# Attention and experts in one kernel: values stored block by block, shorter tables, and adding transfers placed after a gather

## Chip, cores and metric

The kernel runs on one core of a Trainium2 chip. The metric is device time in microseconds of one execution. The engines are TensorE (PE, with its weight loads as PEld), VectorE (DVE), ScalarE (ACT), GpSimd (POOL) and SyncE (SP), which here only issues transfers.

## What is computed

Windowed attention over 8 batches, 8 heads, 576 positions and 64 dims, and then a mixture of experts over the 4608 tokens, where each of 8 experts takes exactly 576 tokens by global greedy choice:

```python
mask_plain = (rel >= 0) & (rel < 32)                          # heads 0 to 3
mask_dil = (rel >= 0) & (rel < 128) & (rel % 4 == 0)          # heads 4 to 7
attn = softmax(where(mask, q @ k.T / 8, -1e9))
x = (attn @ v).transpose(0, 2, 1, 3).reshape(4608, 512)
logits = x @ w_gate                                           # 8 experts
# all (token, expert) pairs in order of falling logit: a pair is taken
# if the token is free and the expert has fewer than 576 tokens
for e in range(8):
    out[mask_e] = relu(x[mask_e] @ w1[e]) @ w2[e]             # 512 -> 1024 -> 512
```

## The kernel before

**Attention** works in 32 units: 8 batches times two kinds of heads (kind 0 plain, kind 1 dilated) times two halves. For a kind the positions are cut into query blocks (9 of 64 plain, 3 of 48 per residue dilated), each with its key block of 96 or 80 positions, 32 of which overlap the block before. A unit (class `Unit`, from L389) scans scores in bf16 for the row maxima (`scan`, L486, and `most`, L493), makes exact scores with the mask and maxima folded in by table matmuls (`scores`, L503 and L506), takes the exponential on ACT (L456), multiplies by the values (`values`, L514) and normalises on DVE (`weigh`). The result goes to the DRAM tensor `xd`; transposes (L564) and matmuls make the gate logits.

The values stand in SBUF with keys of a block on the partitions: 96 rows by 9 blocks by 4 heads by 65 numbers (plain) and 80 rows by 3 blocks by 4 residues by 4 heads by 65 (dilated). `load_v` (L280) loads them for one batch and kind with two transfers, the first block and then the others, from a DRAM layout by position: each row of a block is one contiguous run of 1040 B (plain) or 4160 B (dilated). `load` (L343) brings queries and keys, in 128 rows; for batch 0 in two halves each, and ACT, DVE or POOL copy the queries into a zero-padded tile.

Tables come by `load_const` (L1450): 0 is the identity and masks in bf16, 1 and 2 are the selection tables `lsel0` and `lsel1` for the two kinds (128 rows, of which `scores` reads 64 plus the number of blocks of the unit: 73 or 76), and call 3 loads three together: the fp32 identity, the bf16 tables of the choices (`tri` and on) and the fp32 tables of the choices (`pri` and on). The choices of a batch (`coarse`, L642) read them.

**Experts** (`moe`) run in 8 rounds. Round r finds the expert that fills next by a search on PE and DVE, lists its tokens, gathers their 512 numbers from `xd` by five indirect transfers on POOL (`gather`, L1250; L1258), transposes them on PE (L1272), and splits them into a high and a low part. GEMM 1 (L1309) and GEMM 2 (L1351) use three products of high and low parts. `weights` (L1144) loads a raw tile of 128 x 512 fp32 and splits it: ACT makes the high part, and DVE the low part by a subtraction. For the pairs in `ADDED`, round 0's w2 and round 1's w1 and w2, ACT writes the negated high part and a POOL-issued transfer adds the raw tile to it (L1169). Eight raw tiles of w1 serve in turn; a one-element memset on POOL (L1150), tied to a gather, holds back part of a round's raw loads.

**Order.** Each phase is written out by a list planner (`Schedule`). Every operation has an engine, a planned cost in ns, dependencies, and a boost that moves its due time; the planner takes the operation that is due first on the engine that is free first, and emits the instructions in that order. Each engine then executes in that order, waiting on semaphores for data. Loads on SP get boosts that fall by 1e6 from one call of `sp` (L303) to the next, so they keep the order in which the program names them; the planner takes a transfer to need its bytes divided by `D_R` = 262 B/ns.

Of the kernel before, what the change touches and what calls it, by code (L numbers as in the profile page):

```python
# [14 lines left out]
OP = mybir.AluOpType  # L15
# [4 lines left out]
B, H, S, D = 8, 8, 576, 64  # L20
# [4 lines left out]
WIN, DIL = 32, 4  # L25
NB = S // 64
SR = S // DIL
# [4 lines left out]
NM = 5  # L32
# [6 lines left out]
B_L, B_G, B_T, B_X, B_H, B_HL, B_Y, B_S, B_W = 23000, 27000, 15000, 0, 20000, 17000, 28000, -15000, 1500  # L39
RAW1, D_R, NQ, AHEAD_W = 8, 262, (2, 2), (3, 4)  # L40
ADDED, T_A, T_G = (("2", 0), ("1", 1), ("2", 1)), 4500, 4500
# [7 lines left out]
def blocks(kind):  # L49

    if kind == 0:
        return [(64 * c, max(0, 64 * c - 32)) for c in range(NB)]
    return [(48 * c, max(0, 48 * c - 32)) for c in range(3)]
# [3 lines left out]
KB = (96, 80)  # L57
# [98 lines left out]
class Schedule:  # L156
# [8 lines left out]
    def op(self, eng, cost, fn, deps=(), boost=0, lat=0, dma=0, buf=None):  # L165
        x = Op(len(self.ops), eng, cost, fn, deps, boost, lat, dma, buf)
        for d in x.deps:
            d.users.append(x)
        self.ops.append(x)
        return x  # L170
# [72 lines left out]
def attention(tc, ctx, C, load_const, T, xd, Lt, R):  # L243
    nc = tc.nc
# [5 lines left out]
    op = K.op  # L250
# [27 lines left out]
        return t.rearrange("p (h c a i) -> p h c a i", h=8, c=3, a=2)  # L278

    def load_v(b, kind):  # L280
        n, w, st, q, src = ((96, NB, S, 64, T["in_vp"]), (80, 3, SR, 48, T["in_vd"]))[kind]
        row = src.shape[2]
        t = VT[kind][:n, b % 2]
        t = t.rearrange("p c h d -> p c (h d)") if kind == 0 else t.rearrange("p c r h d -> p c (r h d)")
        o = src.offset + b * st * row
        nc.sync.dma_start(t[:, 0], bass.AP(tensor=src.tensor, offset=o, ap=[[row, n], [1, row]]))
        nc.sync.dma_start(t[:, 1:], bass.AP(tensor=src.tensor, offset=o + (q - 32) * row,
                                            ap=[[row, n], [q * row, w - 1], [1, row]]))


    users = {}
# [10 lines left out]
    first = [1e8]  # L302

    def sp(cost, fn, deps, bytes_, b):
        first[0] -= 1e6
        return op("SP", 475 * cost, fn, deps, first[0], dma=bytes_ / D_R)

    def const(i):
        ready["c", i] = sp(1 if i < 3 else 3, lambda: load_const(i), (), 128 * 1500, 0)

    ready = {}

# [68 lines left out]
    class Unit:  # L381
# [37 lines left out]
        def op(self, eng, cost, fn, deps, boost=0, buf=None):  # L419
            return op(eng, cost, fn, deps, boost - self.u * P_U, buf=buf)  # L420
# [222 lines left out]
    def coarse(c0, c1, x, late):  # L643
        for c in range(c0, c1):
            g, used, use_ = PRE.take()
            f = op("DVE", 290, lambda c=c, g=g: R.coarse(c, g), [x, *used], late)
            counted[0] = op("PE", 60, lambda c=c, g=g: R.coarse_counts(c, g), [f, ready["c", 3], counted[0]], late)
            use_.append(counted[0])

    def tokens(un):  # L650
# [39 lines left out]
    counted = [None]  # L690
# [28 lines left out]
    load(0, 1, 1)  # L719
    load_values(0, 1)  # L720
    const(3)

    def gate_weights():
        nc.gpsimd.memset(wgp, 0.0)
# [386 lines left out]
def moe(tc, ctx, C, R, xd, w1, w2, out):  # L1111
# [33 lines left out]
    def weights(n, r, f, deps):  # L1145

        raw, old, use = RAW[n].take()
        if n == "1" and r < len(AHEAD_W) and f == AHEAD_W[r]:

            gate[r] = op("POOL", 100, lambda: nc.gpsimd.memset(raw[:1, :1], 0.0), [got[r, 1], *old], B_G)  # L1150
        if r in gate:
            deps = [*deps, gate[r]]

        def load():
            if n == "1":
                src = w1[bass.ds(E[r], 1), f].rearrange("o p d f -> p (o d f)")
            else:
                src = w2[bass.ds(E[r], 1), f * 128:f * 128 + 128, :].rearrange("o p d -> p (o d)")
            nc.sync.dma_start(raw, src)

        ld = op("SP", 60, load, [*deps, *old], dma=T_W)
        h, oldh, useh = WH[n].take()
        l, oldl, usel = WL[n].take()
        hi = op("ACT", 525, lambda: act(h, raw), [ld, *oldh], B_W)
        if (n, r) in ADDED:
            use.append(hi)
            ne = op("ACT", 525, lambda: nc.scalar.activation(l, h.bitcast(F32), AF.Copy, scale=-1.0), [hi, *oldl], B_W)
            useh.append(ne)
            lo = op("POOL", 1040, lambda: nc.gpsimd.dma_start(l, raw, accum_op=OP.add), [ne], B_W, lat=T_A)  # L1169
            use.append(lo)  # L1170
        else:
            lo = op("DVE", 600, lambda: sub(nc.vector, l, raw, h), [ld, hi, *oldl], B_W)
            use += [hi, lo]
        useh.append(lo)
        return h, l, hi, lo, useh, usel
# [239 lines left out]
def layout(inputs):  # L1415

    q, k, v, w1, w2 = (np.asarray(inputs[n]) for n in ("q", "k", "v", "moe_w1", "moe_w2"))
    plain = lambda x: x[:, :4].reshape(B, 2, 2, S, D).transpose(0, 1, 4, 2, 3).reshape(B, 128, 2, S)
    dilated = lambda x: x[:, 4:].reshape(B, 4, SR, 2, 2, D).transpose(0, 4, 5, 1, 3, 2).reshape(B, 128, 4, 2, SR)
    ones = lambda x: np.concatenate([x, np.ones(x.shape[:-1] + (1,), x.dtype)], -1)  # L1420
    cb, _, cf, _ = consts()
    rows = np.where(np.arange(24 * 4 * (D + 1)) % (D + 1) == D, 1e-9, 0.0).astype(np.float32)
    d = {
        "in_qp": plain(q), "in_kp": plain(k),
        "in_qd": dilated(q).reshape(B, 128, 8, SR), "in_kd": dilated(k),
        "in_vp": ones(v[:, :4].transpose(0, 2, 1, 3)).reshape(B, S, 4 * (D + 1)),
        "in_vd": ones(v[:, 4:].transpose(0, 2, 1, 3)).reshape(B, SR, DIL * 4 * (D + 1)),
        "in_moe_w_gate": np.asarray(inputs["moe_w_gate"]),
        "in_moe_w1": w1.reshape(NE, DM // 128, 128, FF // 128, 128).transpose(0, 3, 2, 1, 4),
        "in_moe_w2": w2,  # L1430
        "in_cb": cb, "in_cf": cf, "in_rows": np.stack([rows, np.ones_like(rows)]),
    }
    return {n: np.ascontiguousarray(a) for n, a in d.items()}


def load_consts(tc, pool, T):

    nc = tc.nc
    _, ob, _, of = consts()
    cb, cf = T["in_cb"], T["in_cf"]  # L1440
    C, parts = {}, []
    cuts = [(cb, BF, ob, "ident", "lsel0"), (cb, BF, ob, "lsel0", "lsel1"), (cb, BF, ob, "lsel1", "rsel0"),
            (cf, F32, of, "identf", "pri"), (cb, BF, ob, "tri", None), (cf, F32, of, "pri", None)]
    for i, (src, dt, o, n0, n1) in enumerate(cuts):
        c0, c1 = o[n0][0], (o[n1][0] if n1 else src.shape[1])
        t = pool.tile([128, c1 - c0], dt, name=f"const{i}")
        parts.append((t, src[:, c0:c1]))
        C.update({n: t[:, x - c0:x - c0 + w] for n, (x, w) in o.items() if c0 <= x < c1})

    def load_const(i):  # L1450
        for t, src in parts[i:i + 1] if i < 3 else parts[3:]:
            nc.sync.dma_start(t, src)

    load_const.where = ob
    return C, load_const
# [29 lines left out]
```

## Time and profile before

| | us |
|---|---|
| median of three runs (704.57 to 706.64) | 705.41 |
| the profiled execution's own time | 708.44 |
| its span, first to last instruction | 706.6 |
| PE busy (6579 matmuls; 6581 weight loads are PEld) | 665.0 |
| PEld busy | 585.0 |
| DVE busy | 484.7 |
| ACT busy | 291.4 |
| POOL busy | 140.6 |
| moved by DMA, mean | 104.60 MB, 148 GB/s |

Attention fills the span up to about 206 us, the search of the first expert the stretch to about 240, and the rounds the rest. PE is busy 94% of the span, so the gaps of PE and the stretches at a lower granted clock are what to look for. A matmul's end is modelled, so a busy PE is not a PE at its peak. A time of 2.35 in brackets behind an instruction is the idle time of its engine just before it, with what ended it.

### The profile page before, as it was taken

Reading aid. Unit: us, or ns where it says so; the run is one execution under the profiler, and the core shown is the slowest. Engines: PE = TensorE matmul, PEld = TensorE weight load, DVE = VectorE, ACT = ScalarE, POOL = GpSimd, SP = SyncE. Lnnn points to the kernel's source line nnn. Section 1 sums busy time; section 2 is a strip of 40 time slices with the busy share of each in tenths; the row PEclk is TensorE's granted clock in tenths of the full one; section 3 lists DMA queues with packets and bytes.
Section 4 is the critical chain, followed back from the end, with each engine's and each line's share of the span. In section 5 each row is a group of like instructions: output and inputs, shape, how many; then the busy total and the mean of one; then the engine's idle time right before and its main releaser. Section 6 shows DMA issues by size and latency. Waiting matters only on the chain.

```text
span 706.6 us, 17388 instructions
## 1 busy us (share of the span) xinstructions
PE 665.0 (94%) x6579; PEld 585.0 (83%) x6581; DVE 484.7 (69%) x2086; ACT 291.4 (41%) x616; POOL 140.6 (20%) x206
## 2 busy tenths in 40 slices
PE   7899999999974899899999999999999999999995
PEld 5787899888963698699889889879978988988983
DVE  5467877789457889588689879969978854724200
ACT  3344554453521474286335434423524525424210
POOL 6111111100000332452410410310321131211011
PEclk9999999999985899999999999999999999999998
DMA  9999999973211684889314514512711574113001
GB/s 253 266 265 284 279 311 255 264 202 80 63 41 45 194 177 112 249 174 268 98 53 137 180 51 130 185 43 73 239 51 53 164 261 147 50 58 98 1 23 45
DMA packets 58524, 104.60 MB, mean 148 GB/s; under 512 B 6212, under 2 KB 27844, under 8 KB 58436
## 3 DMA queue, kind: packets, MB, share of 16 engines
q1 hardware_dynamic: 49096, 78.32, 38.7%
q0 software_dynamic: 9344, 25.17, 13.4%
q8 instruction: 51, 0.84, 0.5%
q14 instruction: 33, 0.27, 0.1%
HBM read 78.31 MB, written 18.87 MB: 138 GB/s over the span
## 4 chain that ended last, share of the span: by engine, by line
PE 68%; issue 12%; DVE 10%; POOL 3%; DMA 3%; ACT 1%; another core or an unknown queue 1%; POOLq 0%; SPq 0%; DVEq 0%
PE py L1351 18%; PE ph L1309 17%; PE pS L506 9%; PE px L514 6%; PE px L564 3%; PE pS L503 3%; PE pm L486 2%; PE ptx L1272 2%; PE pz L782 2%; PE py L1354 1%; PE py L1356 1%; POOL out L1377 1%; DVE hb L1329 1%; DVE G L796 1%; DMA qs<-in_qd 1%
## 5 line engine op out<-in xcount | busy, mean ns | idle before, releaser
L1351 PE MATMUL py<-w2h,hb 128*128 128x512 f32 x512 | 172.0, 401 | 0.0
L1309 PE MATMUL ph<-xh,w1h 128*128 128x256 f32 (+1 forms) x512 | 138.1, 300 | 0.0
L1309 PE MATMUL ph<-xl,w1h 128*128 128x256 f32 (+1 forms) x512 | 136.8, 298 | 0.0
L1309 PE MATMUL ph<-xh,w1l 128*128 128x256 f32 (+1 forms) x512 | 136.0, 296 | 0.0
L1351 PEld LDWEIGHTS py<-w2h,hb 128*128 128x128 f32 x512 | 96.7, 189 | 19.4
L1351 PE MATMUL py<-w2l,hb 128*128 128x512 f32 x256 | 100.2, 392 | 0.0
L1141 ACT ACTIVATE hb<-ph 128x256 fp32r<-128x256 f32 (+2 forms) x192 | 59.6, 345 | 88.5 <-PE ph L1309 86.9
L1309 PEld LDWEIGHTS ph<-xh,w1h 128*128 128x128 f32 x512 | 91.8, 190 | 0.5
L1309 PEld LDWEIGHTS ph<-xh,w1l 128*128 128x128 f32 x512 | 91.8, 190 | 0.1
L1309 PEld LDWEIGHTS ph<-xl,w1h 128*128 128x128 f32 x512 | 91.4, 190 | 0.1
L506 PE MATMUL pS<-q,k 128*80 128x96 f32 (+1 forms) x672 | 83.0, 265 | 0.0
L1377 POOL DMA_INDIRECT out<-y,idx x40 | 41.3, 1034 | 194.6 <-ACT y L1141 136.0
L456 ACT ACTIVATE E<-pS 96x384 f32<-96x384 f32 (+1 forms) x96 | 46.5, 486 | 75.2 <-PE pS L506 74.1
L1329 DVE SCALAR_TENSOR_TENSOR hb<-ph,hb 128x320 fp32r<-128x320 f32 (+1 forms) x128 | 57.0, 452 | 29.4 <-ACT hb L1141 25.2
L506 PEld LDWEIGHTS pS<-q,k 128*80 128x80 f32 (+1 forms) x672 | 68.5, 158 | 0.0
L1141 ACT ACTIVATE y<-py 128x512 f32<-128x512 f32 (+1 forms) x40 | 23.8, 596 | 104.0 <-PE py L1351 90.5
L493 DVE CUSTOM_DVE_ANT_0 junkm<-pm,const 128x80 bf16<-128x80 f32 (+1 forms) x336 | 59.5, 244 | 4.2 <-PE pm L486 3.6
L1351 PEld LDWEIGHTS py<-w2l,hb 128*128 128x128 f32 x256 | 48.6, 190 | 8.5
L514 PE MATMUL px<-v,E 81*64 81x65 f32 (+1 forms) x1344 | 47.9, 225 | 5.3 <-issue 2.9
L1258 POOL DMA_INDIRECT xg<-xd,idx x40 | 42.1, 1054 | 52.7 <-PE ph L1309 25.1
L514 PEld LDWEIGHTS px<-v,E 81*64 81x64 f32 (+1 forms) x1344 | 42.8, 138 | 10.2 <-issue 3.8
L1141 ACT ACTIVATE w1h<-raw 128x512 fp32r<-128x512 f32 x64 | 39.6, 628 | 27.6 <-DMA raw<-in_moe_w 27.2
(179 smaller groups left out, 1009.5 us busy)
## 6 DMA issues: line engine op xcount, KB each, us to landing
raw<-in_moe_w SPq DMA_DIRECT2D x128, 256.0 KB, 4.6
v<-in_vp SPq DMA_DIRECT2D x8, 780.0 KB, 14.2
v<-in_vd SPq DMA_DIRECT2D x8, 650.0 KB, 10.3
xd<-xs SPq DMA_DIRECT2D x16, 288.0 KB, 7.5
xd<-xs SPq DMA_DIRECT2D x32, 144.0 KB, 9.2
w2l<-raw POOLq DMA_DIRECT2D x16, 256.0 KB
qs<-in_qp SPq DMA_DIRECT2D x7, 576.0 KB, 10.1
k<-in_kp SPq DMA_DIRECT2D x7, 576.0 KB, 9.7
```

The source lines that it names most:

```text
L456: e = self.op("ACT", 380, lambda j=j, pS=pS: nc.scalar.activation(self.E[:self.nk, j * self.gs:j * self.gs + self.gs], pS.tile[:, :self.gs ...
L493: nc.vector.tensor_tensor_reduce(out=jk[:, c - c0, :nk], in0=pm[:, (c - c0) * nk:(c - c0 + 1) * nk], in1=mm[:, min(1, (c if self.kind == 0 ...
L503: nc.tensor.matmul(pS[:nk, c - c0], ls[:64 + n, c], self.r[:64 + n, :2 * nq], start=(c == c0), stop=False, skip_group_check=True)
L506: nc.tensor.matmul(pS[:nk, c - c0], self.Ks[c], self.Qm[c], start=False, stop=True, skip_group_check=True)
L514: nc.tensor.matmul(px[64 * a:64 * a + 64, c - c0], lh, self.V[c][a], start=True, stop=True)
L564: nc.tensor.transpose(t[:, c], src, C["identf"])
L1141: act = lambda o, i, f=AF.Copy: nc.scalar.activation(o, i, f)
L1258: nc.gpsimd.indirect_dma_start(out=xg[:n], out_offset=None, in_=xd, in_offset=bass.IndirectOffsetOnAxis(ap=box[0][:n, m:m + 1], axis=0))
L1309: nc.tensor.matmul(o, a[:, d * 128:d * 128 + 128], b[:, d, c0:c1], start=((d, i) == pairs[0]), stop=((d, i) == pairs[-1]))
L1329: hl = op("DVE", 335 if j == 0 else 400, lambda: nc.vector.scalar_tensor_tensor(hb[:, CAP + c0:CAP + c1], o, 0.0, hb[:, c0:c1], op0=OP.max ...
L1351: nc.tensor.matmul(py, x, w, start=(f + i == 0), stop=(f == NF - 1 and i == 2))
L1377: s = nc.gpsimd.indirect_dma_start(out=out, out_offset=bass.IndirectOffsetOnAxis(ap=box[0][:n, m:m + 1], axis=0), in_=y[:n], in_offset=None)
```

## The change

`load_v` reads values that the host stores per batch as (row of the block) x (block, head, number), so a row of all blocks is contiguous in DRAM: the plain load becomes two transfers, of blocks 0 to 4 and of blocks 5 to 8, and the dilated load one. The bytes are the same. Tables 1 and 2 are loaded in 80 rows. Call 3 loads only the fp32 identity; the tables of the choices become call 4, whose boost puts it behind the six load calls of the second batch (batch 1), and the planned bytes and costs of the table loads are changed. In the experts, an adding transfer of round 1's w1 depends in the plan on the last of that round's five gathers.

```diff
def load_v(b, kind):
-        n, w, st, q, src = ((96, NB, S, 64, T["in_vp"]), (80, 3, SR, 48, T["in_vd"]))[kind]
-        row = src.shape[2]
+        n, src = ((96, T["in_vp"]), (80, T["in_vd"]))[kind]
         t = VT[kind][:n, b % 2]
-        t = t.rearrange("p c h d -> p c (h d)") if kind == 0 else t.rearrange("p c r h d -> p c (r h d)")
-        o = src.offset + b * st * row
-        nc.sync.dma_start(t[:, 0], bass.AP(tensor=src.tensor, offset=o, ap=[[row, n], [1, row]]))
-        nc.sync.dma_start(t[:, 1:], bass.AP(tensor=src.tensor, offset=o + (q - 32) * row,
-                                            ap=[[row, n], [q * row, w - 1], [1, row]]))
+        t = t.rearrange("p c h d -> p (c h d)") if kind == 0 else t.rearrange("p c r h d -> p (c r h d)")
+        w = t.shape[1]
+        cut = (0, w // NB * 5, w) if kind == 0 else (0, w)
+        for o0, o1 in zip(cut, cut[1:]):
+            nc.sync.dma_start(t[:, o0:o1], src[b, :, o0:o1])
...
     def const(i):
-        ready["c", i] = sp(1 if i < 3 else 3, lambda: load_const(i), (), 128 * 1500, 0)
+        ready["c", i] = sp(1, lambda: load_const(i), (), (120e3, 135e3, 150e3, 64e3)[i], 0)
...
-            counted[0] = op("PE", 60, lambda c=c, g=g: R.coarse_counts(c, g), [f, ready["c", 3], counted[0]], late)
+            counted[0] = op("PE", 60, lambda c=c, g=g: R.coarse_counts(c, g), [f, ready["c", 4], counted[0]], late)
...
     const(3)
+
+    ready["c", 4] = op("SP", 950, lambda: load_const(4), (), first[0] - 6.5e6, dma=390e3 / D_R)
...
-            lo = op("POOL", 1040, lambda: nc.gpsimd.dma_start(l, raw, accum_op=OP.add), [ne], B_W, lat=T_A)
+
+            behind = [got[r, NM - 1]] if n == "1" else []
+            lo = op("POOL", 1040, lambda: nc.gpsimd.dma_start(l, raw, accum_op=OP.add), [ne, *behind], B_W, lat=T_A)
...
+    by_block = lambda x, kind: np.concatenate([x[:, k0:k0 + KB[kind]] for _, k0 in blocks(kind)], 2)
...
-        "in_vp": ones(v[:, :4].transpose(0, 2, 1, 3)).reshape(B, S, 4 * (D + 1)),
-        "in_vd": ones(v[:, 4:].transpose(0, 2, 1, 3)).reshape(B, SR, DIL * 4 * (D + 1)),
+        "in_vp": by_block(ones(v[:, :4].transpose(0, 2, 1, 3)).reshape(B, S, 4 * (D + 1)), 0),
+        "in_vd": by_block(ones(v[:, 4:].transpose(0, 2, 1, 3)).reshape(B, SR, DIL * 4 * (D + 1)), 1),
...
     def load_const(i):
-        for t, src in parts[i:i + 1] if i < 3 else parts[3:]:
-            nc.sync.dma_start(t, src)
+        rows = 128 if i not in (1, 2) else 80
+        for t, src in parts[i:i + 1] if i < 4 else parts[4:]:
+            nc.sync.dma_start(t[:rows], src[:rows])
```

## Rows read from the trace of the kernel before

**Rows 1.** Windows: start:end, length, busy us (count) by engine, clock, DMA share, GB/s.
```profile
20.70:26.00 5.30, 5.25 (x57) 4.76 (x58) 3.18 (x29) 0.94 (x2) 0.00 (x0) 0.68 1.05 332
26.00:62.00 36.00, 32.92 (x558) 30.05 (x556) 22.71 (x159) 17.07 (x35) 3.97 (x6) 1.00 1.06 267
62.00:200.00 138.00, 137.98 (x2308) 124.06 (x2308) 101.52 (x685) 66.78 (x128) 9.93 (x15) 1.00 0.77 204
282.00:296.00 14.00, 10.87 (x72) 8.49 (x72) 7.99 (x34) 3.04 (x5) 8.19 (x12) 0.97 0.88 221
```

**Rows 2.** PE's timeline, head: start, us, engine, line, operation, tiles, [idle, releaser].
```profile
20.73 0.57 PE L514 MATMUL px<-v,E 97*64 97x65 f32 x12 [2.35 <-ACT E L456]
33.31 0.45 PE L514 MATMUL px<-v,E 81*64 81x65 f32 x7 [0.71 <-issue]
33.69 0.56 PE L486 MATMUL pm<-k,q 128*128 128x96 bf16 x9
```

**Rows 3.** ACT's timeline of the same stretch.
```profile
19.62 0.68 ACT L272 ACTIVATE q<-qs 64x576 f32<-64x576 f32 x1 [2.87 <-DMA qs<-in_qd]
27.41 0.68 ACT L272 ACTIVATE q<-qs 64x576 f32<-64x576 f32 x1 [0.25 <-DMA qs<-in_qp]
```

**Rows 4.** SP's timeline: issue of the dilated queries' second half.
```profile
11.09 0.35 SPq L354 DMA_DIRECT2D qs<-in_qd  x1
```

**Rows 5.** Windows of the head; DMA share and GB/s stand last.
```profile
8.00:12.00 4.00, 2.83 (x33) 2.54 (x32) 2.35 (x18) 1.92 (x4) 3.73 (x8) 1.00 1.11 221
14.00:16.00 2.00, 1.98 (x45) 1.84 (x42) 1.31 (x5) 1.01 (x2) 0.00 (x0) 1.00 1.14 398
17.00:20.00 3.00, 1.38 (x29) 1.09 (x27) 1.89 (x21) 0.38 (x1) 0.00 (x0) 1.00 1.03 222
22.00:25.00 3.00, 3.00 (x28) 3.00 (x26) 2.36 (x26) 0.49 (x1) 0.00 (x0) 0.50 1.03 393
```

**Rows 6.** DMA issues by tensor: issues, KB each, us from issue to landing.
```profile
const<-in_cb SPq DMA_DIRECT2D x1, 240.0 KB
const<-in_cb SPq DMA_DIRECT2D x1, 216.0 KB, 3.5
```

**Rows 7.** POOL's timeline around round 1's gathers.
```profile
278.61 0.88 POOL L1169 DMA_DIRECT2D w1l<-raw  x1
281.34 0.85 POOL L1169 DMA_DIRECT2D w1l<-raw  x1 [0.54 <-ACT w1l L1167]
283.84 1.03 POOL L1258 DMA_INDIRECT xg<-xd,idx  x1 [0.30 <-DVE A L1053]
288.96 0.91 POOL L1258 DMA_INDIRECT xg<-xd,idx  x1 [0.30 <-issue]
```

**Rows 8.** Busy time in four stretches around round 1's gathers.
```profile
280.00:284.50 4.50, 4.50 (x37) 3.60 (x36) 4.11 (x17) 2.67 (x6) 3.38 (x5) 1.00 1.04 185
284.50:291.00 6.50, 6.50 (x47) 5.20 (x46) 2.69 (x10) 1.74 (x2) 5.24 (x8) 1.00 0.72 215
295.00:299.50 4.50, 4.03 (x21) 3.25 (x18) 3.15 (x12) 1.55 (x3) 0.00 (x0) 0.62 1.02 383
299.50:302.00 2.50, 2.50 (x22) 1.78 (x21) 1.50 (x9) 2.45 (x6) 0.99 (x3) 1.00 0.11 43
```

**Rows 9.** PE's first use of a low part; an add in the chain.
```profile
304.92 0.64 PE L1309 MATMUL ph<-xh,w1l 128*128 128x256 f32 x4
...
315.00 5.70 DMA w2l<-raw
```

**Rows 10.** A later stop of PE for issue, and the page's instruction queue.
```profile
59.85 0.57 PE L514 MATMUL px<-v,E 81*64 81x65 f32 x12 [1.29 <-issue]
...
q8 instruction: 51, 0.84, 0.5%
```

**Rows 11.** Timelines of DVE and PE behind round 1's gathers.
```profile
292.63 0.32 DVE L819 STREAM_TRANSPOSE Q<-pz 128x128 f32<-128x128 f32 x1 [3.65 <-remote]
294.78 0.46 PE L782 MATMUL pz<-G,ohr 128*128 128x64 bf16 x9 [2.66 <-DVE G L796]
```

## The prediction

> **What bounds the kernel now.** I read the stages first: busy time, granted clock and DMA rate of each engine over stretches of the span [rows 1]. Between 62 and 200 us TensorE (PE) shows 137.98 of 138 us busy at the full clock. From 26 to 62 us it lacks 3.08 us, and before that it waits for loads. So an earlier load can pay in the first 26 us or so; later it meets a full PE. The second place with a gap is 282 to 296 us, where PE is busy 10.87 of 14 us: the end of the first expert round and the start of the second.
>
> Next I read PE's own timeline at the head [rows 2]: one stall of 2.35 us ends at 20.73, when ScalarE (ACT) delivers an exponential E. ACT's timeline says why E is late [rows 3]: ACT sat 2.87 us until the second half of the dilated queries landed at 19.6, and that copy stands ahead of E in its queue. SP's queue issued that load at 11.09 [rows 4], so it took 8.5 us. [...] The stretch 20.7 to 26 us has a mean of 0.68, so the clock costs 5.3 x 0.32 = 1.7 us there [rows 1]. Stall and clock together are 4.05 us: all that the head can give before other waits come up.
>
> Last I read what the loads do meanwhile [rows 5]: DMA share is above 1 throughout, but the rate is not one number. With plain values in flight (8 to 12 us) it is 221 GB/s, with dilated values (17 to 20) 222, between them 398, and in the query and key loads of 22 to 25 us 393.
>
> **Values block by block.** The bytes stay: 96 x 9 x 1040 = 899 kB plain and 80 x 3 x 4160 = 998 kB dilated per batch. Contiguous runs grow from 1040 to 5200 and 4160 B (plain) and from 4160 to 12480 B (dilated), and SP issues one transfer fewer per dilated load. If length of run is what slows the values, the plain load goes from 899/221 = 4.1 us to 899/393 = 2.3 us, a gain of 1.8 us ahead of the late queries. But the dilated values already have runs of 4160 B and move at 222 GB/s, no faster than the plain ones with a quarter of that [rows 5]. What the two share, against the fast loads of 128 rows, is 96 and 80 rows, and that stays. I take 0.3 us, near the lower end (0), and keep 1.8 for the range. That the first five blocks now land by themselves can help only the first group of the first unit; the stall sits behind it. Past 62 us the edit is free either way, since PE is full [rows 1].
>
> **Fewer rows of tables.** Of two tables 80 instead of 128 rows are loaded: 216 KB becomes 135, 240 becomes 150 [rows 6]. At 393 GB/s for both forms 175 kB less is 0.45 us. If 80-row loads run at the 222 GB/s of the other 80-row load, 292 kB take 1.31 us against 467/393 = 1.19 us: a loss of 0.12. I take the middle, 0.2 us.
> [...]
>
> **Tables of the choices behind the second batch.** Two tables, together the 390e3 bytes that the diff gives the planner, leave the place ahead of batch 1. At 393 to 222 GB/s batch 1's loads come 1.0 to 1.8 us sooner, batch 2's at the same bytes as before. Value: nothing. Batch 1's queries land at 27.4 (ACT waits 0.25 us there, [rows 3]) and PE first scans them at 33.69 [rows 2]; the 0.71 us that PE lost just before stands as issue, not as a load. The tables themselves are first read far behind 40 us. If this cover were gone, the edit would be worth at most those 1.8 us, and a loss of as much for batch 2 is hidden by the full PE.
>
> **Plan.** Engine orders are written by a list planner. It now believes three tables to cost 0.65 us less in all and the fourth 1.4 us less (192,000 bytes each before, 262 B/ns, and two SP slots of 475 ns), so it may reorder neighbours everywhere. The trace can't price that; I allow 2 us both ways.
>
> **Adds behind the gather.** POOL issues three adding transfers of round 1 at 278.6 to 282.2, then five gathers from 283.84 to 289.87 [rows 7]. The adds fill DMA from 280 to 284.5 (share 1.04, 185 GB/s); the gathers run at share 0.72 behind them [rows 8]. A gather waits for its indices, not for POOL, and they come 1.26 us apart by POOL's issue, so at most the first one's data (its issue ends at 284.87) loses some tenths to the adds. PE has matmuls of round 0 for all of 284.5 to 291 (6.50 of 6.50 us busy, [rows 8]). Gain: 0 to 0.5 us, taken as 0, under that cover. Moved behind, all three adds (0.9 us of POOL each) queue up at 289.9, with a scatter of round 0 (L1377) behind them, and three raw buffers come free that much later for round 2's loads. They then end near 293 on POOL, and at the 5.7 us that an add took to land [rows 9] by about 299. PE first multiplies by such a low part at 304.92 [rows 9]: 6 us of slack. On DMA they add 4.5 us of work to the weight loads of 292 to 299.5; the gap of 2.5 us behind it (share 0.11, [rows 8]) takes half. Cost on the path: 0.
>
> **Sum.** Head 0.5 us, rest 0. Against the profiled execution: 708.44 (span 706.6 and 1.84 around it) - 0.5 = 707.9. The median of the runs is 3.03 lower than that execution, so the forecast is 705.41 - 0.5 = **704.9 us**.
>
> **Rivals.**
> 1. The head stall goes. If long runs do free the values, the queries land up to 2.25 us sooner (1.8 + 0.45), and with the stall shrunk so far the clock need not fall: 1.8 + 1.7 = 3.5 us, 701.9. For it: PE lost 1.29 us at 59.85 without a fall of the clock after it [rows 1, 10], so a shorter stall may pass. Against: equal rates at 1040 and 4160 B.
> 2. The round-1 stall goes. VectorE (DVE) waited 3.65 us for something the profile can't name and PE then stood 2.66 us for DVE [rows 11]; the clock fell after it (0.62 over 295 to 299.5, 1.7 us, [rows 8]). If the adds' traffic causes that and ordinary runs have it, 2.7 + 1.7 = 4.4 us: 701.0. Against: DMA share is 0.72 in just that stretch, and the median lies 3 us below the profiled execution, as if the stall were that execution's own.
> 3. Slower: instruction fetch. PE stops for issue inside its densest runs of short matmuls, 0.71 us at 33.31 and 1.29 at 59.85 [rows 2, 10], while values load; a DMA queue brings the instructions in 51 packets [rows 10]. A dilated run takes 4160 B at 222/16 = 13.9 B/ns, 0.30 us; the new one 0.90. From 26 to 62 us PE runs 1114 instructions [rows 1], at 13160/51 = 258 a packet four fetches; 0.6 us more for each is 2.4 us: 707.8. It decides where a fetch arrives with less than 0.6 us in hand. [...]
> 4. Slower: the late adds meet the weight loads, 4.5 - 2.5 = 2 us late, or the marker write (L1150) that frees SP's next loads ends up behind the adds; if ACT then stands at a conversion ahead of its copies of the gathered rows, PE stands too, and 2 us with a clock drop of 1.7 give 705.4 + 3.7 = 709.1.
> 5. The edits do nothing: PE covers all, 705.4.
>
> **How the numbers follow.** What this kernel's runs can tell from no change is about 0.3%, 2.1 us. Forecast 0.50 (of it 0.08 beyond 2.1 us faster and 0.04 slower, by the planner's 2 us), rival 1 0.18, rival 2 0.12, rival 3 0.10, rival 4 0.06, rival 5 0.04. Faster: 0.08 + 0.18 + 0.12 = 0.38; slower 0.04 + 0.10 + 0.06 = 0.20; within 0.3%: 0.42. The forecast's own range is 702.6 to 707.2; to leave out no more than 2 in 10 it must reach most of rival 1 and rival 3: 701.0 to 708.5.
>
> **What would show it.** Right: dilated queries still land past 18.5, the stall at 18.4 stays over 1.5 us and the clock falls after it; rates with values in flight stay near 220 GB/s; gathers start at the same distance from their indices. Rival 1: rates near 390 with values in flight, no half clock before 26 us. Rival 2: no unnamed DVE wait behind the gathers. Rival 3: more than 3 us of issue waits of PE before 62 us. Rival 4: ACT waiting for weights between 297 and 305. The prediction is wrong if the time moves by over 2.1 us, and its reasons are if it moves less but by such changes cancelling.

## The result and the profile after

The changed kernel takes 711.52 us (median of 20 runs, 706.6 to 719.42) against 704.52 us for the kernel before (median of 20 runs beside them, 700.48 to 708.67). The ratio is 1.0098, with a 95% interval of 1.0078 to 1.0119: 6.9 us slower, outside the range of 701.0 to 708.5. Ratios, here and below, compare only the executions in the faster of two states, so they are not quite the quotients of the medians given beside them.

The profiled execution of the changed kernel is its slowest one, 719.42 us (span 717.6), 7.9 us above its median; that of before was 3.9 above its own. A good part of their difference is therefore spread, and it shows early: attention ends (its last product with the values starts) at 207.5 us here and at 200.5 in before, but in the profiles of the experiments below that have before's attention unchanged it ends anywhere from 197.4 to 207.5. So the comparison is by stages, not by ends. The stage that matters runs from the first product with a gathered row of round 1 to the first matmul of that round's second product. Both stand in PE's timeline; columns are start, us, engine, line, operation, tiles:

```profile
296.32 0.63 PE L1275 MATMUL ptx<-const,xg 128*128 128x128 f32 x4
...
344.87 0.39 PE L1354 MATMUL py<-w2h,hb 128*128 128x512 f32 x1
```

That is 48.6 us. In before it was 43.8, with the stall of 2.66 us of [rows 11] inside it.

The busy times, in the columns of [rows 1], first of the attention and then of this stretch:

```profile
26.00:62.00 36.00, 32.83 (x528) 30.55 (x525) 21.45 (x148) 17.16 (x33) 3.96 (x6) 0.94 1.03 258
62.00:200.00 138.00, 136.31 (x2187) 120.34 (x2186) 99.60 (x679) 64.75 (x123) 10.09 (x15) 0.98 0.79 206
...
291.00:296.00 5.00, 5.00 (x31) 3.82 (x29) 3.06 (x11) 1.76 (x2) 3.93 (x4) 1.00 0.42 130
300.00:320.00 20.00, 19.84 (x166) 17.44 (x165) 15.20 (x58) 14.50 (x29) 11.95 (x15) 1.00 1.09 255
320.00:325.00 5.00, 3.43 (x26) 3.23 (x25) 0.00 (x0) 0.00 (x0) 0.00 (x0) 1.00 1.06 213
325.00:330.00 5.00, 2.17 (x8) 2.17 (x9) 2.48 (x13) 4.21 (x11) 1.71 (x2) 0.71 0.67 183
330.00:335.00 5.00, 4.01 (x20) 3.85 (x19) 4.62 (x22) 2.35 (x6) 1.70 (x2) 0.50 0.84 146
```

In the attention PE lacks 0.1 and 1.7 us more than in [rows 1], and the clock 2 to 6%; that belongs to the spread just named. In the stage, the change does what it says ahead of the gathered rows: from 291 to 296 the DMA share is 0.42, and PE is full there. POOL's timeline has the moved adds right behind the gathers:

```profile
296.63 0.95 POOL L1261 DMA_INDIRECT xg<-xd,idx  x1 [0.31 <-issue]
...
298.93 3.68 POOL L1172 DMA_DIRECT2D w1l<-raw  x4
```

The price comes 25 us later. From 300 to 320 DMA is full (1.09); from 320 to 325 VectorE (DVE), ScalarE (ACT) and POOL do nothing at all, and PE runs dry: of the 15 us from 320 to 335 it lacks 5.39 us, at a clock that then falls to 0.71 and 0.50.

The chain of work that ended last, in the same stretch (start, us, what), names who was late:

```profile
307.56 10.16 DMA w2l<-raw
...
317.84 7.66 DMA raw<-in_moe_w
325.52 0.64 ACT w2h L1142
```

An add of a low part takes 10.16 us to land, where [rows 9] has 5.70. The raw tile that it frees is needed by SP's fifth load of the second weights, which is issued at 317.84 and takes 7.66 us. ACT's, DVE's and PE's timelines, one fence each, show what that does:

```profile
317.24 0.37 ACT L1142 ACTIVATE hb<-ph 128x256 fp32r<-128x256 f32 x1
325.52 0.63 ACT L1142 ACTIVATE w2h<-raw 128x512 fp32r<-128x512 f32 x1 [7.92 <-DMA raw<-in_moe_w]
326.72 0.53 ACT L1142 ACTIVATE hb<-ph 128x320 fp32r<-128x320 f32 x2
```

```profile
327.28 0.49 DVE L1332 SCALAR_TENSOR_TENSOR hb<-ph,hb 128x320 fp32r<-128x320 f32 x1 [8.88 <-ACT hb L1142]
```

```profile
323.03 0.28 PE L1312 MATMUL ph<-xh,w1l 128*128 128x256 f32 x1
323.15 0.28 PE L1312 MATMUL ph<-xl,w1h 128*128 128x256 f32 x1
327.83 0.63 PE L1312 MATMUL ph<-xh,w1h 128*128 128x320 f32 x1 [4.39 <-DVE hb L1332]
328.26 0.47 PE L1312 MATMUL ph<-xh,w1l 128*128 128x320 f32 x1
```

ACT's copies of the first product (`hb<-ph`) stand in its queue behind the conversion of that late weight (`w2h<-raw`). ACT waits 7.92 us, nearly all of it with a copy ready to go (PE ended the next result at about 318.4), DVE waits 8.88 us for a copy, and its own queue holds the next steps of the search. PE finds its result tiles still full and stands 4.39 us, then starts again at a clock of 0.50 (0.47 us for a matmul of 320 columns, where it was 0.31 before). No matmul of the second product is near: PE was still in the first.

### The profile page after: what moved, and what is told of

It reads as the page before. It is cut to its first block, busy times and chain, and to the rows that moved or that the text cites. A ratio compares the mean times of both kernels' runs of the same rounds, so it can differ in the third digit from the quotient of the medians.

```text
span 717.6 us, 17364 instructions
## 1 busy us (share of the span) xinstructions
PE 675.7 (94%) x6578; PEld 593.4 (83%) x6580; DVE 485.0 (68%) x2086; ACT 292.7 (41%) x616; POOL 141.3 (20%) x206
## 4 chain that ended last, share of the span: by engine, by line
PE 66%; issue 12%; DVE 10%; DMA 6%; POOL 3%; ACT 1%; SPq 0%; POOLq 0%; DVEq 0%; ACTq 0%
PE ph L1312 16%; PE py L1354 16%; PE pS L505 9%; PE px L513 6%; PE px L563 3%; PE pS L502 3%; PE pm L485 2%; DMA raw<-in_moe_w 2%; PE ptx L1275 2%; POOL out L1380 1%; DMA w2l<-raw 1%; DVE hb L1332 1%; PE px L596 1%; PE pz L783 1%; PE py L1357 1%
## 5 line engine op out<-in xcount | busy, mean ns | idle before, releaser
L1312 PE MATMUL ph<-xh,w1h 128*128 128x256 f32 (+1 forms) x512 | 140.0, 304 | 4.4 <-DVE hb L1332 4.4
L1312 PE MATMUL ph<-xl,w1h 128*128 128x256 f32 (+1 forms) x512 | 138.3, 301 | 0.0
L1312 PE MATMUL ph<-xh,w1l 128*128 128x256 f32 (+1 forms) x512 | 137.6, 299 | 0.0
L1312 PEld LDWEIGHTS ph<-xh,w1h 128*128 128x128 f32 x512 | 93.3, 193 | 5.2 <-DVE hb L1332 4.6
L1312 PEld LDWEIGHTS ph<-xh,w1l 128*128 128x128 f32 x512 | 93.3, 193 | 0.1
L1312 PEld LDWEIGHTS ph<-xl,w1h 128*128 128x128 f32 x512 | 92.9, 193 | 0.1
L505 PE MATMUL pS<-q,k 128*80 128x96 f32 (+1 forms) x672 | 84.7, 268 | 0.0
L505 PEld LDWEIGHTS pS<-q,k 128*80 128x80 f32 (+1 forms) x672 | 70.2, 161 | 0.0
L1142 ACT ACTIVATE y<-py 128x512 f32<-128x512 f32 (+1 forms) x40 | 23.9, 596 | 103.7 <-PE py L1354 91.9
L513 PEld LDWEIGHTS px<-v,E 81*64 81x64 f32 (+1 forms) x1344 | 43.8, 140 | 10.7 <-issue 6.8
```

What stands on the lines that cost most here:

```text
L505: nc.tensor.matmul(pS[:nk, c - c0], self.Ks[c], self.Qm[c], start=False, stop=True, skip_group_check=True)
L513: nc.tensor.matmul(px[64 * a:64 * a + 64, c - c0], lh, self.V[c][a], start=True, stop=True)
L1142: act = lambda o, i, f=AF.Copy: nc.scalar.activation(o, i, f)
L1312: nc.tensor.matmul(o, a[:, d * 128:d * 128 + 128], b[:, d, c0:c1], start=((d, i) == pairs[0]), stop=((d, i) == pairs[-1]))
```

## The experiments

All times are medians of 9 to 12 runs (of 20 for the changed kernel), each beside its own runs of before (17 to 35), whose medians went from 704.46 to 707.89 us from one set to the next; the ratio is to those, with its 95% interval. "Stage" is the stretch above. "Fifth" is the start of ACT's fifth conversion of a second weight of round 1, counted from the stage's begin, and "wait" is ACT's longest wait for a second weight of round 1, the fifth or a later one, both in the one profiled execution.

| kernel | ratio to before | stage, us | fifth, us | wait, us |
|---|---|---|---|---|
| before | | 43.8 | 23.5 | 2.4 |
| changed | 1.0098 [1.0078, 1.0119] | 48.6 | 29.2 | 7.9 |
| adds alone | 1.0080 [1.0051, 1.0110] | 47.0 | 29.0 | 7.1 |
| blocks alone | 1.0011 [0.9979, 1.0044] | 41.8 | 20.6 | 2.1 |
| choices' tables alone | 1.0007 [0.9976, 1.0037] | 41.9 | 20.1 | 4.5 |
| rows alone | 1.0015 [0.9985, 1.0044] | 41.7 | 20.8 | 3.0 |
| changed, adds not moved | 1.0019 [0.9980, 1.0058] | 45.0 | 24.0 | 1.3 |
| three adds, half | 0.9985 [0.9954, 1.0016] | 43.3 | 24.4 | 2.1 |
| three adds, tiny | 0.9973 [0.9944, 1.0003] | 43.3 | 24.0 | 2.9 |
| adds alone, six tiles | 1.0061 [1.0019, 1.0102] | 47.4 | 22.3 | 5.2 |
| two adds | 1.0060 [1.0031, 1.0090] | 46.0 | 26.6 | 5.7 |
| two extra transfers | 1.0051 [1.0017, 1.0084] | 44.7 | 25.1 | 5.7 |
| tiny adds, ahead | 0.9996 [0.9962, 1.0029] | 42.3 | 19.8 | 3.6 |
| three on DVE | 1.0034 [1.0001, 1.0066] | 40.0 | 21.7 | 1.8 |
| adds, later conversions | 0.9954 [0.9926, 0.9981] | 41.9 | 27.1 | none |
| the same again | 0.9975 [0.9940, 1.0009] | 39.1 | 24.7 | 0.3 |
| before, later conversions | 0.9993 [0.9956, 1.0030] | 43.1 | 26.6 | none |
| three on DVE, later conversions | 0.9995 [0.9969, 1.0021] | 40.4 | 23.9 | none |
| changed, later conversions | 0.9990 [0.9958, 1.0023] | 39.2 | 24.4 | 0.3 |
| adds, fifth to eighth later only | 0.9992 [0.9960, 1.0024] | 41.0 | 28.1 | 0.3 |

The stages of before, of the changed kernel with its adds not moved and of before with later conversions hold a stall of PE of 2.7 to 2.8 us at the gather, which comes up again further down.

### Which part

Each part alone on the kernel before. The adds (TensorE's, VectorE's and SP's orders stay those of before):

```diff
-lo = op("POOL", 1040, ..., [ne], B_W, lat=T_A)
+behind = [got[r, NM - 1]] if n == "1" else []
+lo = op("POOL", 1040, ..., [ne, *behind], B_W, lat=T_A)
```

> The kernel before with one edit: the adding transfers of w1's low parts in later rounds wait for that round's last gather. TensorE's order is the same as before. Theory 'adds' (the four to eight adds, bunched behind the gathers, take DMA from the weight loads, so the weights of round 1's second product land late): 709 to 711.5 us, with ScalarE waiting 5 us or more for raw weights and TensorE standing 4 to 6 us between 295 and 330. Theory 'head and plan' (the added time comes from the value loads, their instruction fetches and the rewritten order of the attention): 704.5 us within 1, no new stall there. The prediction had 0 for it.

Measured: 710.99 us, ratio 1.0080. The others are the new `load_v` with its layout; the split of the third table call; and `t[:rows], src[:rows]` with 80 rows:

> The kernel before with the values alone laid out block by block; the order of every compute engine is that of before. Theory 'adds': 704 to 705, no effect. Theory 'longer runs hold up instruction fetches': 706 to 708, with over 5 us of issue waits of TensorE before 130. Theory 'longer runs free the values' (the prediction's first rival): 701 to 703, rates near 390 GB/s with values in flight. The prediction: rates near 220 GB/s, 0.3 us gained.

> The kernel before with the choices' tables alone moved behind the second batch's loads, with all rows; this also changes the planner's order of the attention (TensorE 168 lines of difference). Theory 'adds': 704.5 within 1. Theory 'plan' (a rewritten order of the attention's groups costs): 706 to 709, with a TensorE gap between 26 and 206 that before does not have. Theory 'early batch 1 pays': 703.

> The kernel before with only 80 of 128 rows of two tables loaded; every engine's order is that of before. By the prediction 0.2 us earlier queries (bounds -0.12 and 0.45), so 704.3 and within the spread. If all partitions' rates count alike, the first of the two tables frees about 0.2 us; if an 80-row load moves at the 222 GB/s of the values, nothing or 0.1 us lost. The look is for the duration of the two 80-row loads beside that of the 128-row ones of before.

Measured: 706.81, 706.69 and 705.83 us beside 705.68 for before. None of the three differs measurably from before; the adds do, by 0.80% of the 0.98%. In ACT's timeline of the run with the adds alone stands the wait of the changed kernel, and in PE's the stop that follows:

```profile
313.18 0.38 ACT L1141 ACTIVATE hb<-ph 128x256 fp32r<-128x256 f32 x1
320.69 0.63 ACT L1141 ACTIVATE w2h<-raw 128x512 fp32r<-128x512 f32 x1 [7.12 <-DMA raw<-in_moe_w]
```

```profile
323.00 0.64 PE L1310 MATMUL ph<-xh,w1h 128*128 128x320 f32 x1 [3.07 <-DVE hb L1330]
```

The windows of the head, of the blocks alone first and then of the fewer rows alone (GB/s last), and ACT's copy of the dilated queries' second half in the same two:

```profile
8.00:12.00 4.00, 4.00 (x33) 3.93 (x32) 1.29 (x8) 1.66 (x3) 3.73 (x8) 0.61 0.99 241
17.00:20.00 3.00, 2.19 (x46) 1.91 (x43) 2.64 (x26) 1.21 (x3) 0.00 (x0) 1.00 0.94 198
```

```profile
8.00:12.00 4.00, 3.24 (x36) 2.70 (x34) 2.62 (x20) 2.14 (x4) 3.73 (x8) 1.00 1.07 237
17.00:20.00 3.00, 0.62 (x22) 0.48 (x18) 1.83 (x15) 1.04 (x2) 0.00 (x0) 1.00 1.01 204
```

```profile
19.28 0.68 ACT L272 ACTIVATE q<-qs 64x576 f32<-64x576 f32 x1 [1.72 <-DMA qs<-in_qd]
```

```profile
18.96 0.68 ACT L272 ACTIVATE q<-qs 64x576 f32<-64x576 f32 x1 [2.97 <-DMA qs<-in_qd]
```

With runs up to five times as long the values still move at 198 to 241 GB/s. The copy starts at 19.28 and 18.96, against 19.62 [rows 3]; in the fourteen profiles with before's loads it starts between 18.82 and 20.82, so neither gain can be told from the spread.

The changed kernel without its moved adds (`behind = []`) closes the sum:

> The changed kernel with the adds left where they were (no wait for the gather); its other three parts stay. Theory 'adds alone': 705.5 to 707.5 us, 4 to 6 us under the changed kernel, and about 42 us from the first product with a gathered row of round 1 to the first of its second product (48.6 in the changed kernel). Rival 'the parts add up in the head as well': 708 or more.

Measured: 707.49 beside 707.89, ratio 1.0019.

### What of the adds

Is it the bytes or the order? The three adds that moved (f = 0, 1, 2) with half of their columns, and with 16 of 512 (these two kernels leave the rest of those low parts out):

```diff
-lo = op(... nc.gpsimd.dma_start(l, raw, accum_op=OP.add), ...)
+lo = op(... nc.gpsimd.dma_start(*((l[:, :256], raw[:, :256]) if n == "1" and f < 3 else (l, raw)), accum_op=OP.add), ...)
```

> The kernel before with the adds behind the gather, and the three adds that moved (f = 0, 1, 2 of round 1) carry half of their columns, so those three low parts are left half unfinished; every engine's order is that of the run with the adds alone. Theory 'DMA work' (the 0.79 MB of three adds enter a stretch in which DMA is full until the second product's weights are in): half of the loss stays, 707.5 to 709 us, 44 to 45.5 us from the first gathered row's product to the second product (47.0 with whole adds, 41.7 to 41.9 where they are not moved). Rival 'order' (what waits is POOL's queue, the raw tiles or SP's order, whatever the size): 710 to 711.5 and 47.

> As the half one, with 16 of 512 columns in each of the three moved adds (those three low parts stay unfinished). Theory 'DMA work': nearly all of the loss is gone, 704.5 to 706.5 us and 41.5 to 43 us between the two products. Rival 'order': 710 to 711.5 and 47.

Measured: 707.24 and 706.73 beside 707.89; both stages 43.3. The order alone costs nothing in the time, so the bytes matter; but half of them cost no more than a thirty-second, which the theory of DMA work had not said. Then more raw tiles for the second weights (`("2", 4)` becomes `("2", 6)`):

> The kernel before with the adds behind the gather and six raw tiles instead of four for the second product's weights. Theory 'DMA work': with DMA full, more tiles let loads start sooner but move no more bytes, so 709 to 711 us. Rival 'ring' (SP's loads of the second product wait for a tile that a late add holds): most of the loss is gone, 705 to 707 us, and the waits of SP's queue for those adds fall from 15.2 us to under 6.

Measured: 711.03, ratio 1.0061, stage 47.4. SP's waits for the adds fell only from 15.2 to 13.9 us, so by its own mark this doesn't exclude the ring, but two more tiles don't mend it: ACT then meets several late weights, one of them (the seventh) 5.2 us late, and PE is busy 0.00 of 5 us in its window from 320 to 325.

Two whole adds moved (`f in (1, 2)`), and, as the counterpart, the adds left where they were and two transfers of the same size added behind the gathers, for nothing:

```diff
             use.append(lo)
+            if n == "1" and f < 2:
+                z = op("POOL", 300, lambda: nc.gpsimd.memset(DUM[f][:, :], 0.0), [got[0, NM - 1]], B_W)
+                use.append(op("POOL", 1040, lambda: nc.gpsimd.dma_start(DUM[f], raw, accum_op=OP.add),
+                              [ld, z, got[r, NM - 1]], 1e6, lat=T_A))
```

> The kernel before with two adds of round 1 (f = 1 and 2) behind the gather, whole; TensorE's order stays. Theory 'DMA work': between half of three (43.3 us from the first gathered row's product to the second product) and all three (47.0), so 44 to 46 us there and 707 to 709.5 in all. Rival 'order or lateness of the last add': as with three, 47 and 710 to 711.

> The kernel before with its adds where they were, plus two further adding transfers of the same size and from the same raw tiles (f = 0 and 1) into unused tiles, issued behind the round's gathers. No low part is late and nobody waits for their result. Theory 'DMA work': the loss of the two moved adds comes without any low part being late, 44 to 46 us and 707 to 709.5. Rival 'lateness of the low parts': no loss, 41.5 to 43 us and 704.5 to 706.

Measured: 709.62 and 709.17 beside 704.46, ratios 1.0060 and 1.0051. POOL's timeline of the second shows the extra transfers, and the wait list of ACT over its stage what they do:

```profile
296.06 1.83 POOL L1174 DMA_DIRECT2D dum<-raw  x2
```

```profile
ACT w2h L1142 <- DMA raw<-in_moe_w: 5.7, 1, 5.7
```

No low part is late in this kernel, and it loses as much as the one with two late low parts. What costs is that DMA carries two more adds there, not that somebody waits for their results. (They also hold two raw tiles of the first weights longer; that was not separated.)

### What the early adds cost

> The kernel before with the three early adds (f = 0, 1, 2 of round 1) cut to 16 of 512 columns where they stand, ahead of the gather (those low parts stay unfinished). What the early adds cost the gather, and so all that moving them can gain: by the prediction 0 to 0.5 us, 704.5 to 705.5. By its second rival (they hold the gathered rows up) 2 to 4 us: 701 to 703, with TensorE standing under 1 us at the gathered rows, where the profiles so far show 0.5 to 3.7 us with the adds ahead.

The three early adds cut to 16 columns where they stand (the rest of those low parts is left out here too): 705.23 beside 704.46, ratio 0.9996. No gain can be seen in the time. In single profiles there is something: in three of the seven kernels with all three adds whole and ahead of the gather (before, [rows 11]; the changed one with adds not moved; before with later conversions) DVE stands 3.7 to 4.0 us for something unnamed right at the gathered rows, and in none of the thirteen others (in two of these, tiny and six tiles, ACT alone waits 3.8 us for something unnamed, and PE does not stop by it). In DVE's timeline of before with later conversions:

```profile
292.67 0.32 DVE L819 STREAM_TRANSPOSE Q<-pz 128x128 f32<-128x128 f32 x1 [3.69 <-remote]
```

The low parts of f < 3 of round 1 by DVE instead of by transfers (`if (n, r) in ADDED and not (n == "1" and f < 3)`):

> The kernel before with the three early low parts subtracted on VectorE instead of added by DMA: no transfer ahead of the gather, none behind it. Theory 'DMA work': 704 to 706, or faster by what the early adds cost the gather (0 to 2 us), unless VectorE's three further operations of 0.6 us lie on the search's chain, then up to 1.8 us slower. About 41 to 42 us from the first gathered row's product to the second product.

Measured: 708.48, ratio 1.0034, in spite of a stage of 40.0. Most of this stands at the very end: from the first matmul of the last second product to the end of the span it is 36.7 us, against 34.5 in the run with fewer rows. PE's part of that is the same (about 25.6 us in both, by its busy windows); but behind POOL's issue of the last scatter the span goes on for 10.1 us, in this kernel and in the one with later conversions below, and for 7.8 to 7.9 in the eighteen others. These 2.3 us are 0.33%. What the end waits for there no profile shows.

### How a late weight becomes lost time

Left open was why half the bytes cost nothing. Either PE lacks the second weights, or ACT stands in front of its copies. The planner was told to expect the last five second weights of round 1 6 us later, and so puts their conversions further back:

```diff
-ld = op("SP", 60, load, [*deps, *old], dma=T_W)
+ld = op("SP", 60, load, [*deps, *old], dma=T_W, lat=6000 if (n, r) == ("2", 1) and f > 2 else 0)
```

> The kernel before with the adds behind the gather, and with the conversions of the fourth to eighth of round 1's second weights planned 6 us later: on ScalarE they stand behind two or three more copies of the first product; the orders of TensorE, VectorE and SP are those of the run with the adds alone. Theory 'ScalarE's queue' (a late weight stops the copies queued behind its conversion): most of the loss goes, 705.5 to 708 us, and 42 to 44.5 us from the first gathered row's product to the second product (47.0 without the later conversions). Rival 'TensorE lacks the weights': 709.5 to 711.5 and 46 to 48.

> The kernel before, adds where they were, with the same later conversions. Theory 'ScalarE's queue': ScalarE waits only 2 to 4.5 us for such weights here and TensorE loses under 1.5 us by it, so 703.5 to 705.5 and 41 to 42 us between the two products. Rival 'TensorE lacks the weights': 704.5 or up to 1 us slower, 42 to 43.

> The kernel before with the three early low parts subtracted on VectorE and the same later conversions, no early add at all. With three adds' traffic gone DMA is least loaded: 39.5 to 41 us between the two products (40.0 without the later conversions). In all 703 to 708: the run without the later conversions gave 0.34% more than before in spite of the shorter stage, which its attention (ended 204.0, range 197 to 204 with the same code) or its last round may explain.

Measured: 703.96, 706.45 and 706.20 beside 706.77. With the adds moved and the conversions later, the loss is not only gone: the kernel is 0.46% faster than before. The same order without moved adds, or with no early adds, gives nothing that can be measured; but the last of these has the longer end just named, and without those 2.3 us it would by estimate stand 0.4% under before. The whole changed kernel with it, and the first of the three once more:

> The changed kernel, all four parts, with the same later conversions of round 1's second weights and nothing else; the orders of TensorE, VectorE and SP are those of the changed kernel. Theory 'ScalarE's queue': ratio to before 0.994 to 1.002 (1.0098 without the later conversions), and 41 to 44 us from the first gathered row's product to the second product (48.6 without). Rival 'the other three parts share the loss': over 1.005.

> The kernel before with the adds behind the gather and the later conversions, a second time beside new runs of before. If the gain is the gather's (no early adds in its way, and no late weight in ScalarE's): 0.993 to 0.999 again. If the first time was the chip's: 0.998 to 1.003.

Measured: 705.92 and 704.34 beside 706.00, ratios 0.9990 and 0.9975. The loss of the changed kernel is mended by ACT's order alone. The gain over before came again with half its size, in an interval that reaches to 1.0009.

One thing remained mixed in: with `lat` the first four conversions come earlier too, so that the fifth load is issued 17.9 us into the stage instead of 21.2. Now only the moment from which the planner lets the fifth to eighth conversion start is moved, nothing ahead of them:

```diff
+        if (n, r) == ("2", 1) and f > 3:
+            ld.rlat = 6000
...
-        return d.end + (d.lat if d.eng == eng else d.lat + self.LAT)
+        return d.end + getattr(d, "rlat", 0) + (d.lat if d.eng == eng else d.lat + self.LAT)
```

> The kernel before with the adds behind the gather, and only the fifth to eighth conversions of round 1's second weights behind three to four more copies on ScalarE. The fifth load should land as late as with the adds alone, about 29 us behind the first gathered row's product. Theory 'ScalarE's queue': no copy of the first product waits behind the conversion, the stage takes 41.5 to 44 us instead of 47.0 and the ratio to before is 0.994 to 1.001. Rival 'the earlier load': the second product still lacks its weights, 46 to 47.5 us and a ratio of 1.004 to 1.009.

Measured: 705.99 beside 704.87, ratio 0.9992, stage 41.0. ACT's timeline of this kernel:

```profile
323.97 0.55 ACT L1141 ACTIVATE hb<-ph 128x320 fp32r<-128x320 f32 x2 [1.38 <-PE ph L1312]
324.41 0.63 ACT L1141 ACTIVATE w2h<-raw 128x512 fp32r<-128x512 f32 x1
```

and its windows from there:

```profile
315.00:320.00 5.00, 5.00 (x45) 4.90 (x44) 3.86 (x15) 3.79 (x9) 3.50 (x5) 1.00 1.12 202
320.00:325.00 5.00, 5.00 (x47) 4.90 (x46) 3.92 (x20) 1.97 (x6) 0.14 (x1) 1.00 1.09 257
325.00:330.00 5.00, 5.00 (x40) 4.96 (x39) 4.63 (x20) 3.26 (x9) 0.92 (x2) 1.00 0.98 266
```

The fifth load is issued 21.6 us into the stage, as late as with the adds alone (it has landed 6.5 us later at the most, where it took 7.8 there); DMA is as full as ever (1.12); the fifth conversion runs 28.1 us into the stage, and nobody waits: PE is busy 15.00 of 15 us. So PE did not lack the weights. ACT's queue turned their lateness into lost time.

The fifth load also explains the half adds. In the four kernels whose adds stay ahead, with nothing added and no stall at the gather (blocks, choices' tables and rows alone; tiny adds, ahead), it is issued 16.0 to 16.4 us into the stage. With the adds behind the gather it is 19.7 for tiny ones, 20.2 for half and 21.2 for whole ones, so the order alone makes most of that delay. But the load then lands 4.3 and 4.2 us later in the first two, and 7.8 us later in the third. Without later conversions ACT is ready for the fifth one 19 to 22 us into the stage (near 24 where the stall at the gather comes first).

Shorter waits of ACT reach PE too, but less of them does. With waits of 1.3 to 4.5 us PE stops for DVE behind the gather, for `hb` or for the search's result `ge`, 0.3 to 2.7 us in all, and no loss can be told in the time. The largest is that of the choices' tables alone:

```profile
323.40 0.19 PE L1029 MATMUL pz<-ge,const 128*128 128x72 bf16 x1 [2.72 <-DVE ge L992]
```

With waits from 5.2 us on these stops come to 3.8 to 5.5 us, and those are the five kernels that lose 0.51 to 0.98%; in four of them the clock falls behind the stop as well (lowest window of 5 us: 0.50 in the changed kernel, 0.80 with the adds alone, 0.60 with six tiles, 0.66 with two adds), in the one with the extra transfers it does not (1.00). With later conversions there are no such stops: PE's waits list none for `hb` or `ge`. With the first product's copies ahead of the conversion a start at 28.1 is harmless.

## Why the prediction was wrong

**The step that failed** is the last one of "Adds behind the gather": "Cost on the path: 0." Its start was right: all three adds queue up behind the gathers, and the late low parts have time (two extra transfers without any late low part cost as much as two late adds). What it left out is everything else that crosses the same stretch. It followed the adds to their first reader at 304.92 and stopped there, and it set 4.5 us of DMA work against the weight loads up to 299.5 and a gap of 2.5 us behind [rows 8]. That gap was for the most part the echo of that execution's own stall: with blocks alone, where there is no such stall, the share from 294 to 304 of its own time is 0.92 (0.78 in before), and what is left of the gap is 1.5 us at 0.43, from 302.5 to 304. Behind it DMA is full up to the second product: in the profile of before its share is 1.09, 1.08, 1.02 and 1.06 in the four stretches from 310 to 330, which were not read. And the second weights' loads wait for tiles which those transfers free (SP waits 14.4 us in four pieces for adds of `w2l` in the changed kernel).

**Rival 4** named the mechanism, late adds that meet weight loads and ACT standing at a conversion ahead of copies, with a chance of 0.06 and 3.7 us. The place was wrong: not 297 to 305 and the copies of gathered rows (ACT waits 2.3 us in five pieces for first weights there and behind), but the fifth second weight and the copies of the first product, 20 us on. The price was short too: 5.2 us of stage (47.0 less 41.8) and 5.6 us in the time (0.80% of 705.68) with the adds alone. Its second half, the marker write behind the adds, wasn't it: in the changed kernel it stands ahead of them on POOL (298.89 against 298.93), and so it does with the tiny adds, which lose nothing.

**Rival 2** was held to be that execution's own stall, and its gain put at 4.4 us. It is neither: the stall came in three of seven profiles with whole adds ahead and in none without, which fits the adds' traffic. With the late weights out of ACT's way the four sets of runs with moved adds stand 0.46%, 0.25%, 0.10% and 0.08% under before (3.2, 1.8, 0.7 and 0.6 us); cutting the early adds down where they stand gave nothing. Of all these only the first is clear of noise, so that moving them can gain rests on it, and how much stays open.

**Values block by block, fewer rows.** 0.5 us was forecast, and nothing of it can be told from the spread. Of its marks two hold: the queries' copy starts past 18.5 (20.07 in the changed kernel), and with values in flight the rate stays at 198 to 241 GB/s at any length of run, against 393 to 398 in 128 rows [rows 5]. So the value taken for long runs, near the lower end, was right, and rival 1 falls. The values' rows stayed at 96 and 80 in every kernel, and the rate did not rise with the runs; that the number of rows sets it was not shown.

The third mark fails: a stall over 1.5 us in that place. In the changed kernel it is gone; PE stands 1.37 us for values instead, up to 13.14, and the clock is 0.50 from 15 to 18. With blocks alone it is 1.19 us, the clock stays at 1.00 behind it, and was 0.61 from 8 to 12. So the stall and the half clock of before (0.50, [rows 5]) moved, and no gain came of it.

**Tables of the choices** and the planner's new order: 1.0007 with half the one and the other. Nothing, as said, and well inside the 2 us allowed.

**Rival 3.** Its mark, over 3 us of issue waits of PE before 62, is met in the changed kernel: 3.2 us. But the long runs don't set it: with blocks alone these waits come to 2.1 us, with the adds alone, whose loads are before's, to 3.7, and with the extra transfers, also with before's loads, to 3.6. The mark was too weak; before itself stands at 2.9. That a fetch waits behind one run on one of 16 engines (the 222/16 of the prediction) was the author's estimate; no run shows it.

Of the sum's terms one is thus shown wrong: it was 0 and measures 5.6 us. The others are not contradicted, but the 0.5 us of the head lies below what these runs can tell.

## What to carry to other kernels

A transfer that is moved off one path must be priced against everything that DMA carries from its new place to the next deadline, not only against its own reader (two extra transfers that nobody reads cost 0.51% here); read the DMA share all the way there, and in an execution without a stall of its own. Then ask which in-order queue meets the late data: a conversion that waits for a load holds back whatever is written behind it (7.92 us in the changed kernel), and putting it behind the copies that are ready cost nothing that these runs can tell (ratio 0.9992). A planner that moves a transfer has to be told the later landing as well; here 6 us on the landing, with the adds moved, took the whole loss away and gave the fastest kernel of all, 0.46% under the kernel before in one set of runs and 0.25%, within its noise, in the next.

## What the runs showed of the hardware

- Lost time was not in proportion to the traffic. Three adds moved with half of their bytes cost nothing that can be told, two whole ones 0.60%. What counts is what reaches PE: with waits of ACT up to 4.5 us it stopped for DVE up to 2.7 us, with waits from 5.2 us on 3.8 to 5.5 us, and behind the stall of 4.39 us the clock was 0.50, which adds to the loss.
- Much of the spread of before's time, 699 to 716 us over all sets, is there when attention ends: in sixteen profiles with one and the same order of attention that is between 197.4 and 207.5 us. The windows from 40 to 62 of the kernel with half adds (end at 197.4) and of the one with the adds alone (202.9) show PE full in the one and 3.11 us short in the other, with the same loads and the same order:

```profile
40.00:62.00 22.00, 22.00 (x406) 20.38 (x403) 17.62 (x144) 9.84 (x20) 1.99 (x3) 1.00 1.06 275
```

```profile
40.00:62.00 22.00, 18.89 (x333) 17.30 (x333) 13.97 (x105) 9.43 (x19) 1.99 (x3) 1.00 1.06 255
```
